# Strassen's seven block products for the first product of the dense experts

## The chip, the cores and the metric

The kernel runs on one core of a Trainium2 chip, with 1 launch. The metric is device time in microseconds (us); lower is better. TensorE (PE in the rows) multiplies, VectorE (DVE), ScalarE (ACT) and GpSimd (POOL) work beside it, and DMA queues move data between HBM and the on-chip memories SBUF and PSUM. PSUM has eight banks of 512 fp32 values per partition; a matrix product accumulates in one bank.

## What is computed

An attention over 2 x 576 tokens feeds two mixtures of experts. The first one sends each token to two of eight experts. The second one, which is changed here, is dense: each of its four experts works on all 1152 tokens.

```python
def _moe2_ref(x, domain_probs, w1, w2):          # x (1152, 512), w1 (4, 512, 1024), w2 (4, 1024, 512)
    p = domain_probs / (domain_probs.sum(-1, keepdims=True) + 1e-09)
    out = np.zeros((N, D), dtype=np.float32)
    for e in range(E):
        h = np.maximum(x @ w1[e], 0.0)
        out += p[:, e:e + 1] * (h @ w2[e])
    return out
```

## The kernel before

Every fp32 operand of a product is held as two parts of type fp32r, a high part (the rounded value) and a low part (the rest). A product is the sum of three: high by high, low by high and high by low. The second mixture keeps its tokens transposed, `xh2` and `xl2`, 128 partitions by 4 pieces of the inner size by 1152 tokens. The arrangement of tokens in nine groups of 128 is called c, and the eight pieces of 128 of the hidden size f.

For each dense expert e there are two stages. The first product (lines 907 to 924) takes 24 steps, 8 pieces f by 3 stretches t of 384 tokens. A step is 12 matmuls of 384 columns into one PSUM bank (L922: 4 inner pieces by 3 products of parts), then ScalarE writes the high part of the ReLU (L923, `h2h`) and VectorE the low part (L924, `h2l`), both reading PSUM. The pool `psg` gives three banks to these steps. The second product (lines 927 to 952) takes nine steps, one for each c: 24 matmuls of 512 columns (8 f by 3, L937), in one of the two banks of `psy`, and one VectorE instruction that adds the result, times the token's weight, to `acc` (L940 for the first expert, L942 for the others). For the last expert GpSimd then sends the rows to the output with an indirect DMA (L946); the last group is cut in two halves of 256 columns.

Weights arrive by `wchunk` (L94): a load of 256 KB into one of five buffers `raw` on SyncE's queue, a cast to the high part on ScalarE (L99), and a subtraction for the low part on GpSimd or VectorE (L102). `w1chunk` has eight buffers (`w1c`), `w2chunk` has eight (`w2c`). The chunks of `w1` for expert e+1 are asked for in the second product of expert e.

The dense expert 0 is special. Its tokens are not all there when it starts: for groups 3 to 8 `fetch` (L713) gathers the two rows that the first mixture left in HBM, into buffers `raw`, with indirect DMAs of GpSimd; `combine` (L726) adds them on VectorE to `x2`; `turn_x2` (L733) transposes a group on TensorE and splits it into `xh2` and `xl2`. These twelve pieces of work stand one by one in front of the first twelve steps of expert 0 (lines 908 to 914), and that expert goes through t in its outer loop, so that tokens 0 to 383 come first.

Each engine works through its own queue in order and waits at the head for what an instruction needs. The order in a queue is set when the program is built, by a planner that takes an instruction early where it holds it ready; it is not always the order of the code.

Of the kernel before, what the change touches and what calls it, by code (L numbers as in the profile page):

```python
# [27 lines left out]
def tile_attention_moe_moe(  # L28
# [65 lines left out]
    def wchunk(src, pool, tag, hi, lo):  # L94
        raw = rawp.tile([P, 512], F32, tag="raw", name="raw")
        nc.sync.dma_start(raw if len(src.shape) == 2 else raw.rearrange("p (k f) -> p k f", k=KC), src)
        t = pool.tile([P, 2, 512], F32R, tag=tag, name=tag)
# [6 lines left out]

    def w1chunk(src, f, hi, lo):
        return wchunk(src[:, f * P:(f + 1) * P].rearrange("(k p) f -> p k f", p=P), w1p, "w1c", hi, lo)
# [400 lines left out]
    psg = ctx.enter_context(tc.tile_pool(name="psg", bufs=3, space=PSUM))  # L507
    psy = ctx.enter_context(tc.tile_pool(name="psy", bufs=2, space=PSUM))
    pstr = ctx.enter_context(tc.tile_pool(name="pstr", bufs=2, space=PSUM))
# [203 lines left out]
    def fetch(c):  # L713
        for k2 in range(2):
            i = 2 * c + k2
            if c > 2:
                ygs[i] = rawp.tile([P, DM], F32, tag="raw", name="yg")
# [71 lines left out]
    for e in range(E1):  # L789
# [69 lines left out]
        for d in range(KC):  # L859
            for f in (2 * d, 2 * d + 1):  # L860
# [30 lines left out]
    uc1 = {0: wc1}  # L891
# [3 lines left out]
    hh = x2p.tile([P, FC, NT * P], F32R, name="h2h")  # L895
    hl = x2p.tile([P, FC, NT * P], F32R, name="h2l")
    acc = x2
    puts = []
    for e in range(E2):
        wc1 = uc1.pop(e)  # L900

        if e == 0:
            order = [(f, t, 3) for t in (0, 3, 6) for f in range(FC)]
        else:
            order = [(f, t, 3) for f in range(FC) for t in (0, 3, 6)]
        wc2 = []
        for i, (f, t, m) in enumerate(order):
            if e == 0 and i < 12:
                if i % 2 == 0:
                    with tc.issue_after(y_adds[0].ins):  # L910
                        fetch(i // 2 + 3)
                        combine(i // 2 + 3)
                else:
                    turn_x2(i // 2 + 3)
            if i % (len(order) // FC) == 0:
                wc2.append(w2chunk(u2[e], len(wc2), nc.scalar, nc.gpsimd))
            o = slice(t * P, (t + m) * P)
            ps = psg.tile([P, 512], F32, tag="g1", name="ps_h2")[:, 0:m * P]
            w = wc1[f].rearrange("p s (k f) -> p s k f", k=KC)
# [90 lines left out]
```

## Time and profile before

| | us |
|---|---|
| median of 3 runs (lowest, highest) | 897.89 (897.16, 898.18) |
| the profiled execution, its own time | 893.92 |
| its span in the trace | 892.1 |
| TensorE busy | 837.3 (94%) |
| VectorE, ScalarE, GpSimd busy | 409.1, 345.0, 343.9 |

The profile is of one execution. A matmul's row in it is longer than the time to the start of the next one, since matmuls overlap; a pace is therefore read from start to start. TensorE's busy time says that it has work, not that it works at its best.

### The profile page before, as it was taken

Reading aid. Unit: us, or ns where it says so; the run is one execution under the profiler, and the core shown is the slowest. Engines: PE = TensorE matmul, PEld = TensorE weight load, DVE = VectorE, ACT = ScalarE, POOL = GpSimd, SP = SyncE. Lnnn points to the kernel's source line nnn. Section 1 sums busy time; section 2 is a strip of 40 time slices with the busy share of each in tenths; the row PEclk is TensorE's granted clock in tenths of the full one; section 3 lists DMA queues with packets and bytes.
Section 4 is the critical chain, followed back from the end, with each engine's and each line's share of the span. In section 5 each row is a group of like instructions: output and inputs, shape, how many; then the busy total and the mean of one; then the engine's idle time right before and its main releaser. Section 6 shows DMA issues by size and latency. Waiting matters only on the chain. (4 is left out here: it accounts for less than half of the span.)

```text
span 892.1 us, 13550 instructions
## 1 busy us (share of the span) xinstructions
PE 837.3 (94%) x5148; PEld 780.3 (87%) x5148; DVE 409.1 (46%) x796; ACT 345.0 (39%) x771; POOL 343.9 (39%) x299
## 2 busy tenths in 40 slices
PE   4899999938979989999999899999999999999996
PEld 3799999938979989999999898899888998899885
DVE  7988888867455435446566521122111221122111
ACT  3778888734325345446432440033103330032100
POOL 6768774647455425334045340052104220040011
PEclk9999999978999989999999999999999999999998
DMA  5423231617446465465373420041103210010011
GB/s 147 112 69 96 70 82 41 181 56 246 144 136 187 141 200 152 141 215 173 116 220 102 136 80 15 0 119 38 34 1 85 58 36 12 1 36 1 12 48 47
DMA packets 94636, 84.42 MB, mean 95 GB/s; under 512 B 14036, under 2 KB 74852, under 8 KB 94564
## 3 DMA queue, kind: packets, MB, share of 16 engines
q1 hardware_dynamic: 89204, 69.34, 26.8%
q0 software_dynamic: 4384, 13.47, 4.7%
q8 instruction: 43, 0.70, 0.3%
q10 hardware_dynamic: 976, 0.66, 0.2%
q14 instruction: 29, 0.24, 0.1%
HBM read 69.66 MB, written 9.66 MB: 89 GB/s over the span
## 5 line engine op out<-in xcount | busy, mean ns | idle before, releaser
L937 PE MATMUL ps_y<-w2c,h2h 128*128 128x512 f32 (+1 forms) x592 | 182.4, 389 | 0.0
L922 PE MATMUL ps_h<-xh,w1c 128*128 128x384 f32 x768 | 149.8, 337 | 3.1 <-DVE h2l L924 3.1
L102 POOL TENSOR_TENSOR w2c<-raw,w2c 128x512 fp32r<-128x512 f32 x60 | 83.0, 1409 | 164.8 <-ACT w2c L99 164.7
L922 PEld LDWEIGHTS ps_h<-xh,w1c 128*128 128x128 f32 x768 | 134.0, 188 | 4.6 <-DVE h2l L924 4.3
L937 PEld LDWEIGHTS ps_y<-w2c,h2h 128*128 128x128 f32 x592 | 110.2, 188 | 25.3
L102 POOL TENSOR_TENSOR w1c<-raw,w1c 128x512 fp32r<-128x512 f32 x60 | 77.3, 1293 | 130.9 <-ACT w1c L99 127.8
L866 PE MATMUL ps_y<-hh,w2c 128*128 128x320 f32 x512 | 124.8, 323 | 2.0 <-PEq L742 2.0
L99 ACT CAST w2c<-raw 128x512 fp32r<-128x512 f32 x96 | 56.4, 619 | 174.3 <-issue 133.6
L937 PE MATMUL ps_y<-w2c,h2l 128*128 128x512 f32 (+1 forms) x296 | 115.2, 389 | 0.0
L924 DVE SCALAR_TENSOR_TENSOR h2l<-ps_h,h2h 128x384 fp32r<-128x384 f32 x96 | 53.3, 557 | 134.5 <-ACT h2h L923 134.5
L923 ACT ACTIVATE h2h<-ps_h 128x384 fp32r<-128x384 f32 x96 | 47.0, 492 | 122.0 <-PE ps_h L922 121.0
L804 PE MATMUL ps_h<-xh,w1c 128*128 128x320 f32 x512 | 89.4, 317 | 3.1 <-DVE hl L806 3.1
L866 PEld LDWEIGHTS ps_y<-hh,w2c 128*128 128x128 f32 x512 | 90.2, 195 | 2.2 <-issue 2.2
L866 PE MATMUL ps_y<-hl,w2c 128*128 128x320 f32 x256 | 82.0, 320 | 3.2 <-DVE x L729 1.7
L804 PEld LDWEIGHTS ps_h<-xh,w1c 128*128 128x128 f32 x512 | 79.4, 193 | 3.9 <-DVE hl L806 3.6
L922 PE MATMUL ps_h<-xl,w1c 128*128 128x384 f32 x384 | 82.4, 336 | 0.0
L942 DVE SCALAR_TENSOR_TENSOR x<-ps_y,tp,x 128x512 f32<-128x512 f32 (+1 forms) x28 | 20.5, 732 | 129.5 <-PE ps_y L937 129.5
L922 PEld LDWEIGHTS ps_h<-xl,w1c 128*128 128x128 f32 x384 | 67.9, 188 | 0.0
L937 PEld LDWEIGHTS ps_y<-w2c,h2l 128*128 128x128 f32 x296 | 55.6, 188 | 12.6
L99 ACT CAST w1c<-raw 128x512 fp32r<-128x512 f32 x88 | 54.2, 616 | 13.6 <-DMA raw<-in_moe_w_dram 13.0
L866 PEld LDWEIGHTS ps_y<-hl,w2c 128*128 128x128 f32 x256 | 50.1, 196 | 4.0 <-DVE x L729 2.0
L293 DVE TENSOR_REDUCE nm<-ps_s 128x1 f32<-128x576 f32 x64 | 48.2, 753 | 10.9 <-PE ps_s L321 10.3
(213 smaller groups left out, 1367.6 us busy)
## 6 DMA issues: line engine op xcount, KB each, us to landing
raw<-in_moe_w_dram SPq DMA_DIRECT2D x192, 256.0 KB
Cs<-C SPq DMA_DIRECT2D x28, 144.0 KB
yd<-yn SPq DMA_DIRECT2D x7, 512.0 KB
xd<-xp SPq DMA_DIRECT2D x4, 576.0 KB
vv<-in_v_dram SPq DMA_DIRECT2D x8, 256.0 KB
qk<-in_q_dram SPq DMA_DIRECT2D x7, 256.0 KB
qk<-in_k_dram SPq DMA_DIRECT2D x7, 256.0 KB
yd<-yn SPq DMA_DIRECT2D x7, 128.0 KB
```

The lines of the kernel that those rows point to most:

```text
L99: hi.copy(t[:, 0, :], raw)
L102: lo.tensor_sub(t[:, 1, :], raw, _f(t[:, 0, :]))
L293: nc.vector.reduce_max(un.nm[:, c:c + 1], ps[:, :, 0:HS], axis=AX.XY, negate=True)
L804: nc.tensor.matmul(ps, w[:, s, kk, :], xx[:, kk, :], start=(n == 0), stop=(n == 3 * KC - 1))
L866: nc.tensor.matmul(ps, wc2[f][:, s, d * P:(d + 1) * P], xx[:, f, :], start=(n == 0), stop=(n == 3 * FC - 1))
L922: nc.tensor.matmul(ps, w[:, s, kk, :], xx[:, kk, o], start=(n == 0), stop=(n == 3 * KC - 1))
L923: nc.scalar.activation(hh[:, f, o], ps, AF.Relu)
L924: vec.scalar_tensor_tensor(hl[:, f, o], ps, 0.0, _f(hh[:, f, o]), op0=ALU.max, op1=ALU.subtract)
L937: nc.tensor.matmul(ps, xx[:, f, c * P:(c + 1) * P], wc2[f][:, s, dd], start=(n == 0), stop=(n == 3 * FC - 1))
L942: vec.scalar_tensor_tensor(acc[:, c, dd], ps, tp[:, c, 8 + e:9 + e], acc[:, c, dd], op0=ALU.mult, op1=ALU.add)
```

## The change

The dense experts 1, 2 and 3 compute their first product by Strassen's scheme in Winograd's form. The matrices are cut in halves: tokens into two halves of 576 (`TH`), the inner size into two of 256, the hidden size into two of 512. Seven products of such blocks and some sums of blocks give the four output blocks. A `unit` takes one piece f and the piece f + 4: 7 products, each of 12 matrix steps (2 inner pieces by 3 products of parts by 2 stretches of 288 tokens), so 84 matmuls of 288 columns. Both stretches go to one PSUM tile of two banks; the pool `psu` has three such tiles, opened when `psg` and `pstr` are closed. The sums of the seven products are made by VectorE in PSUM and in four buffers `tmp`, and one product is copied by ScalarE. There are four units to an expert.

The sums of weights are made by GpSimd in the `raw` buffers (`unit_weights`, four additions of 256 columns) and split as chunks of their own. The sums of tokens are made once, by VectorE, during expert 0 (`token_sums` twice, `token_sum3` twice) and split by ScalarE and VectorE.

The hidden size is now worked off in two sets of two units (`NS` = 2): the first product of a set, then a second product over the set's four pieces, which adds to `acc`. The second product has 12 matmuls to a step, and eighteen steps to an expert. `h2h` and `h2l` have half the size.

Expert 0 keeps its plain first product of 24 steps of 12 matmuls, in the new order of sets: set 0 goes through t in its outer loop with the second product of groups 0 to 2 after the first t. The gathers use the `tmp` buffers and no longer `raw`, the first two before the first step. The low parts of `w2` for expert 0 are made by VectorE and no longer by GpSimd. The last expert of the first mixture asks for the chunks of `w1` in the order 0, 4, 1, 5, 2, 6, 3, 7.

The core of the diff:

```diff
-    for e in range(E2):
-        wc1 = uc1.pop(e)
...
+    def token_sums(q):
+
+        c0, c1 = slice(q * TQ, (q + 1) * TQ), slice(TH + q * TQ, TH + (q + 1) * TQ)
+        b11, b12 = plain(0, c0), plain(0, c1)
+        vec.tensor_tensor(b11, b12, b11, op=ALU.subtract)
+        b22 = plain(2, c1)
+        vec.tensor_tensor(b22, b22, b11, op=ALU.subtract)
+        put_parts(b11, Th[:, 0, :, c0], Tl[:, 0, :, c0])
+        b21 = plain(2, c0)
+        vec.tensor_tensor(b21, b21, b22, op=ALU.subtract)
+        put_parts(b22, Th[:, 1, :, c0], Tl[:, 1, :, c0])
+        put_parts(b21, Th[:, 2, :, c0], Tl[:, 2, :, c0])
...
+    def unit_weights(src, m):
+
+        eng = nc.gpsimd
+        ra, rb = load_raw(w1rows(src, m)), load_raw(w1rows(src, m + FC // 2))
+        lo, hi = slice(0, 256), slice(256, 512)
+        ta, tb = (split_chunk(x, w1p, "w1c", nc.scalar, eng) for x in (ra, rb))
+        eng.tensor_tensor(rb[:, hi], rb[:, lo], rb[:, hi], op=ALU.add)
+        eng.tensor_tensor(rb[:, lo], ra[:, lo], rb[:, lo], op=ALU.subtract)
+        eng.tensor_tensor(ra[:, lo], rb[:, hi], ra[:, lo], op=ALU.subtract)
+        eng.tensor_tensor(ra[:, hi], ra[:, hi], ra[:, lo], op=ALU.subtract)
+        tc_, td_ = (split_chunk(x, w1p, "w1c", nc.scalar, eng) for x in (ra, rb))
...
+        def product(a, b):
+            ps = psu.tile([P, 2, 512], F32, tag="u", name="ps_u")[:, :, 0:TQ]
+            w = blocks[a].rearrange("p s (k f) -> p s k f", k=2)
+            bh, bl = B[b]
+            todo = [(w[:, s, kk], xx[:, kk]) for s, xx in ((0, bh), (1, bh), (0, bl)) for kk in range(2)]
+            for n, (x, y) in enumerate(todo):
+                for j in range(2):
+                    nc.tensor.matmul(
+                        ps[:, j], x, y[:, j * TQ:(j + 1) * TQ], start=(n == 0), stop=(n == len(todo) - 1))
+            return ps
...
+        p1 = temp()
+        nc.scalar.copy(p1, product("11", "11"))
+        both = add(product("S2", "T2"), p1, temp())
+        c11 = add(product("12", "21"), p1)
+        relu_hi(2 * m, h0, c11)
+        v = add(product("S1", "T1"), both, temp())
+        relu_lo(2 * m, h0, c11)
+        p7 = product("S3", "T3")
+        add(p7, both, both)
+        c22 = add(p7, v)
+        relu_hi(2 * m + 1, h1, c22)
+        c12 = add(product("S4", "22"), v)
+        relu_hi(2 * m, h1, c12)
+        relu_lo(2 * m + 1, h1, c22)
+        c21 = add(product("22", "T4"), both)
+        relu_hi(2 * m + 1, h0, c21)
+        relu_lo(2 * m, h1, c12)
+        relu_lo(2 * m + 1, h0, c21)
...
+                if at[0][0] < E2:
+                    prepare = {1: lambda k=at[0]: prepare_unit(k), 4: lambda k=at[1]: prepare_unit(k)}
+            if e > 0:
+                for m in range(MS):
+                    load_w2(2)
+                    unit(m, units.pop((e, s, m)))
+                second(e, s, wc2, range(NT))
+            elif s == 0:
+                for t in (0, 3, 6):
+                    for f in range(2 * MS):
+                        if t == 0:
+                            load_w2(1)
+                        plain_chunk(f, wc1[f], t)
+                        if steps:
+                            steps.pop(0)()
+                    for c in range(3) if t == 0 else ():
+                        second(e, s, wc2, (c,))
+                        steps.pop(0)()
+                    if t == 3:
+                        steps.pop(0)()
+                second(e, s, wc2, range(3, 6))
+                token_sums(0)
+                second(e, s, wc2, range(6, NT))
+            else:
+                for f in range(2 * MS):
+                    load_w2(1)
+                    for t in (0, 3, 6):
+                        plain_chunk(f, wc1[2 * MS + f], t)
+                    if f == 1:
+                        token_sums(1)
+                pctx.close()
+                psu = ctx.enter_context(tc.tile_pool(name="psu", bufs=3, space=PSUM))
+                second(e, s, wc2, range(0, 4))
+                token_sum3(0)
+                second(e, s, wc2, range(4, 7))
+                token_sum3(1)
+                second(e, s, wc2, range(7, NT))
```

In it `TQ` is 288, `NT` is 9, `MS` is 2 and `FC` is 8. `plain` adds a block's high and low parts (one VectorE instruction of 576 columns), `put_parts` splits a sum again (a ScalarE copy and a VectorE subtraction of 576), `add` is a VectorE addition of 576 columns with one operand in PSUM, `relu_hi` and `relu_lo` are the ScalarE and VectorE instructions of L923 and L924 on 576 columns. `prepare` runs after the second product's groups 1 and 4; `second` holds the loop of lines 927 to 952 for one set; `steps` are the `combine` (with the next `fetch`) and `turn_x2` of groups 3 to 8.

## Rows read from the trace of the kernel before

**Rows 1.** Page: the span, busy time by engine, TensorE's granted clock in 40 slices

```profile
span 892.1 us, 13550 instructions
PE 837.3 (94%) x5148; PEld 780.3 (87%) x5148; DVE 409.1 (46%) x796; ACT 345.0 (39%) x771; POOL 343.9 (39%) x299
PEclk9999999978999989999999999999999999999998
```

**Rows 2.** The chain that ended last, in order of time: start, length, what

```profile
583.45 49.92 PE ps_h L922 x288
...
733.68 50.39 PE ps_y L937 x216
```

**Rows 3.** A stretch of expert 1: length, busy time of each engine (instructions), granted clock

```profile
583.90:633.70 49.80, 49.80 (x289) 49.71 (x288) 13.08 (x24) 16.22 (x33) 14.56 (x12) 1.00 0.24 70
```

**Rows 4.** TensorE by time: start, length, what, idle before; two runs of 288 columns

```profile
180.68 0.30 PE L392 MATMUL av<-el,v 128*128 128x288 f32 x1
...
181.60 0.29 PE L394 MATMUL av<-e,v 128*128 128x288 f32 x1
...
182.62 0.29 PE L392 MATMUL av<-el,v 128*128 128x288 f32 x1
...
183.56 0.29 PE L394 MATMUL av<-e,v 128*128 128x288 f32 x1
```

**Rows 5.** VectorE, one line's instructions: ns shortest/median/longest, first and last start

```profile
L924 DVE SCALAR_TENSOR_TENSOR h2l<-ps_h,h2h x96: 542/558/559, 479.2 to 834.6; 128x384 fp32r<-128x384 f32 x96
L729 DVE SCALAR_TENSOR_TENSOR x<-yg,tp,x x18: 732/752/2395, 454.6 to 496.4; 128x512 f32<-128x512 f32 x18
```

**Rows 6.** Groups by line and shape: busy us, mean ns of one, idle before

```profile
L293 DVE TENSOR_REDUCE nm<-ps_s 128x1 f32<-128x576 f32 x64 | 48.2, 753 | 10.9 <-PE ps_s L321 10.3
L294 ACT ACTIVATE eb<-ps_s,nm 128x576 f32<-128x576 f32 x64 | 47.8, 747 | 7.5 <-DVE nm L293 7.4
L222 POOL TENSOR_TENSOR qs<-t,t 128x256 fp32r<-128x256 f32 x1 | 0.7, 726 | 0.7 <-PE ptq L263 0.7
```

**Rows 7.** VectorE by time, in experts 0 and 1

```profile
501.38 1.01 DVE L924 SCALAR_TENSOR_TENSOR h2l<-ps_h,h2h 128x384 fp32r<-128x384 f32 x2
...
587.76 1.02 DVE L924 SCALAR_TENSOR_TENSOR h2l<-ps_h,h2h 128x384 fp32r<-128x384 f32 x2 [3.53 <-ACT h2h L923]
```

**Rows 8.** ScalarE: line L923 in all, then two casts of weights by time

```profile
L923 ACT ACTIVATE h2h<-ps_h x96: 483/492/503, 478.4 to 834.0; 128x384 fp32r<-128x384 f32 x96
491.01 0.62 ACT L99 CAST w2c<-raw 128x512 fp32r<-128x512 f32 x1 [5.03 <-DMA raw<-in_moe_w_dram]
518.92 0.61 ACT L99 CAST w1c<-raw 128x512 fp32r<-128x512 f32 x1
```

**Rows 9.** TensorE by time: expert 0's first product, and where expert 3's ends

```profile
475.38 0.42 PE L922 MATMUL ps_h<-xh,w1c 128*128 128x384 f32 x1
...
479.90 0.60 PE L736 MATMUL pt<-csb,x 128*128 128x128 f32 x4
480.25 0.59 PE L922 MATMUL ps_h<-xl,w1c 128*128 128x384 f32 x2
...
486.17 1.68 PE L922 MATMUL ps_h<-xh,w1c 128*128 128x384 f32 x8 [0.72 <-DVE h2l L924]
...
495.97 1.66 PE L922 MATMUL ps_h<-xh,w1c 128*128 128x384 f32 x8 [1.91 <-DVE h2l L924]
...
532.90 0.39 PE L937 MATMUL ps_y<-w2c,h2h 128*128 128x512 f32 x1
...
833.83 0.39 PE L937 MATMUL ps_y<-w2c,h2h 128*128 128x512 f32 x1
```

**Rows 10.** GpSimd by time: six low parts of weights

```profile
581.84 7.56 POOL L102 TENSOR_TENSOR w2c<-raw,w2c 128x512 fp32r<-128x512 f32 x6
```

**Rows 11.** Stretches in the first mixture, columns as in Rows 3

```profile
326.80:330.40 3.60, 2.13 (x10) 1.75 (x10) 1.19 (x2) 0.94 (x2) 0.00 (x0) 0.65 0.38 142
330.40:334.80 4.40, 4.39 (x17) 4.39 (x18) 0.25 (x1) 0.00 (x0) 0.00 (x0) 0.51 0.21 65
```

More of the change, by code (lines that the diff above doesn't have):

```diff
@@ L716, in fetch @@
             if c > 2:
-                ygs[i] = rawp.tile([P, DM], F32, tag="raw", name="yg")
+                ygs[i] = temp().rearrange("p j t -> p (j t)")[:, 0:DM]
             else:
@@ L890, in tile_attention_moe_moe, with temp @@
     mctx.close()
-    uc1 = {0: wc1}
     x2p = ctx.enter_context(tc.tile_pool(name="x2p", bufs=1))
-    hh = x2p.tile([P, FC, NT * P], F32R, name="h2h")
-    hl = x2p.tile([P, FC, NT * P], F32R, name="h2l")
+    TH = NT * P // 2
+    TQ = TH // 2
+    NS = 2
+    MS = FC // 2 // NS
+    def temp():
+        return x2p.tile([P, 2, TQ], F32, tag="tmp", name="tmp", bufs=4)
     acc = x2
     puts = []
-    for e in range(E2):
-        wc1 = uc1.pop(e)
[L902 to L919, printed above, removed]
-            for n, (s, xx, kk) in enumerate(
-                    [(s, xh2, kk) for kk in range(KC) for s in (0, 1)] + [(0, xl2, kk) for kk in range(KC)]):
-                nc.tensor.matmul(ps, w[:, s, kk, :], xx[:, kk, o], start=(n == 0), stop=(n == 3 * KC - 1))
-            nc.scalar.activation(hh[:, f, o], ps, AF.Relu)
-            vec.scalar_tensor_tensor(hl[:, f, o], ps, 0.0, _f(hh[:, f, o]), op0=ALU.max, op1=ALU.subtract)
-        if e + 1 < E2:
-            uc1[e + 1] = []
-        for c in range(NT):
-            if e + 1 < E2 and c < FC:
-                uc1[e + 1].append(w1chunk(u1[e + 1], c, nc.scalar, nc.gpsimd))
-            cuts = (0, 256, 512) if e == E2 - 1 and c == NT - 1 else (0, 512)
@@ new lines, in relu_hi, with relu_lo, plain_chunk @@
+    def relu_hi(f, o, src):
+        hi = hs[0][:, f, o]
+        nc.scalar.activation(hi if len(src.shape) == 2 else hi.rearrange("p (j t) -> p j t", j=2), src, AF.Relu)
+    def relu_lo(f, o, src):
+        hi, lo = hs[0][:, f, o], hs[1][:, f, o]
+        if len(src.shape) == 3:
+            hi, lo = (x.rearrange("p (j t) -> p j t", j=2) for x in (hi, lo))
+        vec.scalar_tensor_tensor(lo, src, 0.0, _f(hi), op0=ALU.max, op1=ALU.subtract)
+    def plain_chunk(f, w, t):
+        o = slice(t * P, (t + 3) * P)
+        ps = psg.tile([P, 512], F32, tag="g1", name="ps_h2")[:, 0:3 * P]
+        w = w.rearrange("p s (k f) -> p s k f", k=KC)
+        for n, (s, xx, kk) in enumerate(
+                [(s, xh2, kk) for kk in range(KC) for s in (0, 1)] + [(0, xl2, kk) for kk in range(KC)]):
+            nc.tensor.matmul(ps, w[:, s, kk, :], xx[:, kk, o], start=(n == 0), stop=(n == 3 * KC - 1))
+        relu_hi(f, o, ps)
+        relu_lo(f, o, ps)
@@ new lines, in unit, with add @@
+    def unit(m, blocks):
+        def product(a, b):
[8 more added lines that the diff above has]
+            return ps
+        def add(ps, other, dst=None):
+            dst = ps if dst is None else dst
+            vec.tensor_tensor(dst, ps, other, op=ALU.add)
+            return dst
+        p1 = temp()
[16 more added lines that the diff above has]
+        relu_lo(2 * m + 1, h0, c21)
@@ L932, in tile_attention_moe_moe, with second @@
+    def second(e, s, wc2, cs):
+        for c in cs:
+            last = e == E2 - 1 and s == NS - 1
+            cuts = (0, 256, 512) if last and c == NT - 1 else (0, 512)
             for d0, d1 in zip(cuts, cuts[1:]):
```

76 lines of the change are left out of this document (66 added, 10 removed).

## The prediction, made before the changed kernel was run

> **What bounds the kernel now.** I read the page first. TensorE is busy 94% of the span at a granted clock of nine tenths or more nearly everywhere, and no other engine passes 46% [rows 1]. A mean like that hides the stages, so the chain that ended last comes next. In the dense experts it is TensorE and nothing else: the first product of expert 1 is 49.92 us for 288 matmuls, the second one of expert 2 is 50.39 us for 216 [rows 2]. That is 0.173 us for 384 columns and 0.233 us for 512. The stretch of a first product then shows the cover: in 49.80 us VectorE works 13.1 us, ScalarE 16.2 us, GpSimd 14.6 us [rows 3]. So what TensorE saves there is saved in the end, as long as the engines that now get more work keep up.
>
> **Experts 1 to 3, first product.** Removed: 288 matmuls of 384 columns. Added: 4 units of 84 matmuls of 288 columns, 336. The trace has matmuls of 288 columns in runs: seven starts take 0.92 us in one and 0.94 us in another, 0.131 and 0.134 [rows 4]; I take 0.133. 336 x 0.133 = 44.7 us against 49.9: 5.2 us less in each expert, 15.7 us in three. With the two paces as ends the gain is 14.7 to 17.7 us. The second product keeps its matmuls, in 18 groups of 12 (12 x 0.233 = 2.8 us).
>
> **VectorE in the units.** A unit has 11 VectorE instructions of 576 columns, seven additions and four low parts, where 12 of 384 columns (0.558 us [rows 5]) stood for the same two pieces. A reduction of 576 columns out of PSUM took 0.753 us [rows 6], and two L924 in a row take 1.01 us, 0.46 from start to start, 0.1 less than the length of one [rows 7]. So 11 x 0.75 = 8.3 us at most, 7.2 us when packed, beside 84 x 0.133 = 11.2 us of TensorE: it fits in sum, and the question is the order. Four of the 11 write back into PSUM; no row shows that. Nearest is the same read with a result in SBUF, 0.75; below that I see no reason, above it I allow the fixed part once more: from 384 to 576 columns the length grows by 0.195 us, 1.02 ns a column, which leaves 0.558 - 0.39 = 0.17 us for the rest.
>
> With three tiles in `psu`, product n + 3 waits until product n's tile is read out. A product is 12 x 0.133 = 1.6 us, so there are 3.2 us from a product's end to the start of the one that needs its tile. ScalarE starts about 0.2 us after the following matmul's start [rows 8, 9], VectorE 0.1 us after ScalarE's end [rows 5, 8]. Tile 3 is freed by a low part that stands behind the addition on product 4: 1.6 + 0.2 + 0.66 + 0.75 + 0.1 = 3.3 us, 0.1 too late for product 6. The tile of product 5 ends the same way behind the addition on product 6, and delays the next unit's first product by 0.1. At the end of a set, `c21` needs 0.2 + 0.75 + 0.1 + 0.65 (ScalarE's 0.492 for 384, 0.747 for an exponential of 576 [rows 6, 8]) + 0.1 + 0.75 = 2.55 us until its low part is there; the second product wants that after ten matmuls, 2.33 us. So 0.3 + 0.2 = up to 0.5 us for a set of two units. I take 0.4, six sets, 2.4 us. With the dearer PSUM write it is 0.3 more per set (4.2 us in all); if the planner finds something else for TensorE there, nothing.
>
> **ScalarE and GpSimd.** Weights now cost GpSimd 4 subtractions of 512 (7.56/6 = 1.26 us [rows 10]) and 4 additions of 256 (0.73 us [rows 6]) for a unit, 8.0 us, and two low parts of `w2`, 2.5 us: 21 us for a set, which lasts 22.3 + 25.2 = 47.5 us. ScalarE has about 3.3 us of PSUM reads and 6 casts of 0.62, 7 us for a unit. Both are covered. GpSimd's six subtractions ran from 581.84 to 589.40 and VectorE's L924 beside them kept its 1.02 us for two [rows 7, 10]: instructions with one operand in PSUM, as all 11 are, are not held up. Loads are as many as before (8 chunks of `w1`, 8 of `w2` to an expert). Nine more additions to `acc` in each expert, 0.75 us each in groups of 2.8 us, hide in the same way.
>
> **Expert 0.** Its first product runs from 475.38 to 532.90, 57.5 us [rows 9], for 49.9 us of matmuls and 27 transposes at 0.35 us for four [rows 9], 2.4 us. 5.2 us are lost to waits on gathers, loads and VectorE, 0.72 and 1.91 us of them in the two rows shown [rows 9], while ScalarE stood 5.03 us at a cast whose buffer `raw` was late [rows 8]. The change gives the gathers other buffers, issues two before the first step, and puts three groups of the second product (8.4 us) ahead of where tokens 384 and on are wanted. I expect those waits gone. Against that VectorE gets the token sums, 28 instructions of 576 columns, about 0.75 us each, 21 us in all, beside the low parts of `w2`. Ten of them in one go (7.5 us) behind an addition to `acc` would cost what exceeds two groups less an addition, 7.5 - (5.6 - 0.75) = 2.7 us, and ten amid first-product steps 2 us or so (three free banks, 3 x 2.1 us). But the trace shows the planner moving work ahead: a cast of the next expert's `w1` runs at 518.92, inside the first product [rows 8], though the code asks for it in the second. Spread like that the sums cost little. These instructions read SBUF twice; such a one (L729) took up to 2.4 us, against 0.75 as a rule, while GpSimd worked too [rows 5]. So expert 0 lies between 5.2 us gained and 5 us lost; I take 2 us of new waits, 3.2 us gained.
>
> **The end** is unchanged: two halves, an addition and an output DMA each. The DMAs now come every 2.8 us, GpSimd needs about 1 us for one.
>
> **Rivals.** (A) The part work blocks ScalarE. Casts of the weight sums wait for GpSimd's chain (2 subtractions, 4 additions: 2.5 + 2.9 = 5.4 us) at the head of ScalarE's queue, and behind them stand the copy of product 1 and the ReLUs. TensorE has 3.2 us of tiles; beyond that a cast costs up to 2.2 us and more if the cast's load is late too. For it: ScalarE did stand 5.03 us so in expert 0, and TensorE with it [rows 8, 9]. Against it: the work is asked for in the second product, where ScalarE has nothing urgent. At 12 units x 2.2 us = 26 us the kernel would be 10 us slower, 908; it is slower as soon as a unit loses more than (15.7 + 3.2 - 2.4)/12 = 1.4 us. (B) VectorE becomes the bound of the units, if its instructions on PSUM in place take much more than a row shows. At 1 us each for 11 a unit is 11 us and just hides; what it loses in order then is about 0.7 us a unit, 8 us, and the kernel is at 889. At 1.14 us nothing would be left. (C) Weight loads set TensorE's pace. A load lasts longer than a 288-column matmul and TensorE's loads are busy 49.71 of 49.80 us at 384 columns [rows 3]; if a matmul could not start faster than 0.17 us, 336 of them are 57 us, 21 us more in all, 916. The runs at 0.133 had one load for each matmul as well, so I give it little. (D) The clock. In a stretch where TensorE was busy only 2.13 of 3.60 us the granted clock was 0.65, and in the 4.4 us behind it 0.51, the lower level of 1.2 GHz [rows 11]; at the wait of 1.91 us in expert 0 the matmuls behind kept their pace [rows 9]. Waits of 0.1 us are far from that; but units at half the clock would take 11 us more each. The Trainium skill speaks against this change here: "TensorE: Matmul & The Clock Gate", section "A second HAM failure mode: psum-queue depth-cycling", reports a kernel that cycled through PSUM banks, idled briefly between groups and saw its clock fall and rise again and again. By that rule the units could lose up to 12 x 11 us and the kernel would be near 1000; the rows of this case, with three banks cycled in every first product at a clock of 1.00 [rows 3], do not bear it out.
>
> **How the numbers follow.** The sum is -15.7 + 2.4 - 3.2 = -16.5 us. The profiled execution took 893.92 us, with a span of 892.1, and would take 877.4; the median of the runs shown stands 3.97 us above it, and the same difference from 897.89 gives 881.4. Without new waits and with all of expert 0's old ones gone it is -17.7 - 5.2 = -22.9, 875. With the dear writes, the slow pace and 5 us lost in expert 0 it is -14.7 + 4.2 + 5 = -5.5, 892.4. Chances: the forecast (875 to 892.4, in which B's mild form lies) 0.76, A 0.12, of which a quarter ends between 892 and 896, C 0.03, D 0.02, B in the hard form 0.04, faster than 875 0.03. The range 875 to 894 holds about 8 in 10. About 0.2% (1.8 us) is what a measurement of this kernel can tell from no change: faster 0.81, within it 0.03, slower 0.16.
>
> **What would show it.** Right: the distance from the start of a unit's first matmul to the next unit's is near 11.2 us and its matmuls follow each other every 0.13 us; waits of TensorE on VectorE are under 0.3 us; the first to last matmul of an expert takes near 96 us instead of 100.3; expert 0 takes some 105 us instead of 107.9. Wrong: in A the rows of ScalarE's casts have GpSimd as releaser with microseconds behind them; in B VectorE is busy nine tenths or more in the units; in C the matmuls' starts are 0.17 us apart with no wait; in D the granted clock in the units is below 1; and if the token sums run in blocks, expert 0's second product has waits of several us on `acc`.

## The result, and the profile after

The changed kernel takes 908.4 us (median of 4 runs, 907.12 to 910.01), the kernel before on the same chip 897.52 (4 runs, 892.24 to 898.18): 1.0135 times as long, with an interval of 1.0093 to 1.0177. It is slower, by 1.35%. The forecast was 881.4 with a range of 875 to 894; the time is the one that rival A gave, 908.

The page of the changed kernel (span, busy time by engine):

```profile
span 906.1 us, 14046 instructions
...
PE 831.0 (92%) x5280; PEld 767.2 (85%) x5280; DVE 513.3 (57%) x928; ACT 366.5 (40%) x791; POOL 402.8 (44%) x363
```

TensorE does have less to do, 831.0 us for 837.3 [rows 1], and the span is 14.0 us longer: TensorE stands and waits, 8% of the span for 6%. The averages of the other engines are far from full, as before. So the time went into order, not into volume. Split by stage, from the start of one first product to the start of the next (the last stage ends with the span):

| us | before | after |
|---|---|---|
| start of expert 0 | 475.38 | 471.97 |
| expert 0 | 107.9 | 113.1 |
| experts 1 to 3 | 308.8 | 321.0 |
| of it: five sets that prepare another one | | 53.80, 53.54, 52.11, 53.73, 52.39 |
| of it: the last set, with the output | | 55.5 |

What TensorE waited for in experts 1 to 3 (line waited for: us in total, times, longest), then its weight loads, and then ScalarE, of the changed kernel:

```profile
PE ps_y L1039 <- ACT h2h L971: 12.7, 5, 2.6
PE ps_u L1000 <- DVE h2l L977: 5.0, 5, 1.2
PE ps_u L1000 <- ACT tmp L1010: 1.0, 5, 0.3
...
PEld ps_y L1039 <- ACT h2h L971: 15.1, 6, 3.0
...
ACT w1c L105 <- POOL raw L964: 19.4, 10, 3.2
ACT w2c L105 <- DMA raw<-in_moe_w_dram: 15.3, 15, 2.0
```

In the kernel before, this view lists no wait of TensorE there. Now it waits five times for the ReLU (L971) of the last piece, once in each set but the last, five times about 1 us for low parts, and five times some 0.2 us for the copy of product 1 (L1010). ScalarE itself waits ten times for GpSimd's last addition of weights (L964), once for each unit that these experts prepare, and fifteen times for a load of `w2`.

The chain that ended last, in order of time (start, length, what), shows how the one leads to the other at the end of expert 1's first set:

```profile
606.57 0.63 ACT w1c L105
...
607.27 1.30 POOL w1c L108
...
611.10 0.74 POOL raw L964
...
611.86 0.62 ACT w1c L105
612.48 0.55 ACT h2h L971
...
613.53 0.56 ACT h2h L971
...
614.14 22.82 PE ps_y L1039 x90
```

It is to be read as a relay for the next unit's weights: a cast, a subtraction, four additions (three are left out), the next cast. Only then come the two ReLUs that TensorE needs now, with one more cast between them (left out). Before the change the chain was a row of TensorE pieces here [rows 2]. ScalarE's queue a little earlier and at the same place (start, length, what, idle before and its cause):

```profile
597.33 0.62 ACT L105 CAST w2c<-raw 128x512 fp32r<-128x512 f32 x1 [1.94 <-DMA raw<-in_moe_w_dram]
597.85 0.65 ACT L971 ACTIVATE h2h<-ps_u 128x576 fp32r<-128x576 f32 x1
...
606.57 0.62 ACT L105 CAST w1c<-raw 128x512 fp32r<-128x512 f32 x1 [1.79 <-PE ps_u L1000]
...
611.86 0.62 ACT L105 CAST w1c<-raw 128x512 fp32r<-128x512 f32 x1 [3.22 <-POOL raw L964]
612.38 0.64 ACT L971 ACTIVATE h2h<-ps_u 128x576 fp32r<-128x576 f32 x1
```

The cast of 611.86 stands at the head for 3.22 us; the ReLU behind it starts with no wait of its own, so its operand had been there. The relay's first cast, at 606.57, had itself waited 1.79 us for TensorE: the eight buffers `w1c` hold just the two units of the running set (four chunks to a unit), and one came free only then. The cast of 597.33, of `w2`, stood 1.94 us for its load with a ReLU behind it; the low part of that ReLU comes at 598.53 and TensorE, which wants its PSUM tile, has a wait of 1.16 us until 599.43. So there are two casts that block, one behind GpSimd (the 12.7 us on L971), one behind a load (the 5.0 us on L977). TensorE, by time, at the end of the set:

```profile
609.53 0.40 PE L1039 MATMUL ps_y<-w2c,h2l 128*128 128x512 f32 x1
...
611.15 0.40 PE L1039 MATMUL ps_y<-w2c,h2h 128*128 128x512 f32 x1
614.14 0.88 PE L1039 MATMUL ps_y<-w2c,h2h 128*128 128x512 f32 x2 [2.59 <-ACT h2h L971]
...
618.12 0.40 PE L1039 MATMUL ps_y<-w2c,h2l 128*128 128x512 f32 x1
```

Eight matmuls of the second product run, then TensorE waits 2.59 us, and then the next ten take 3.98 us (614.14 to 618.12) where ten at 0.233 take 2.33. The granted clock says why (length, busy time of PE, PEld, DVE, ACT, POOL with instructions, clock, DMA share, GB/s; the second and third line are the 4 us behind the same wait in the next two sets, the last line is the two units of the last set, which prepares nothing):

```profile
614.00:618.00 4.00, 3.86 (x10) 2.99 (x11) 1.51 (x2) 0.09 (x1) 1.06 (x1) 0.57 0.50 131
...
667.59:671.59 4.00, 4.00 (x12) 3.08 (x13) 1.49 (x2) 0.00 (x0) 0.93 (x1) 0.70 0.47 131
721.24:725.24 4.00, 4.00 (x17) 3.11 (x18) 1.60 (x3) 0.00 (x0) 0.93 (x1) 1.00 0.44 131
...
850.81:873.30 22.49, 22.49 (x171) 22.41 (x170) 14.52 (x20) 5.69 (x9) 0.00 (x0) 1.00 0.01 1
```

After this wait TensorE works near its lower level of 1.2 GHz for about four microseconds. Not each such wait brings that: the five waits on the ReLU last 2.54 to 2.59 us, and over the 4 us behind them the clock is 0.57, 0.70, 1.00, 0.69 and 1.00. The two sets in which it stays at 1.00 are the two short ones, 52.11 and 52.39 us. Why an equal wait brings it in one set and not in another, no run here shows. The loss of the first set adds up: its second unit takes 13.03 us (596.50 to 609.53) instead of 11.2, 1.83 (of which the wait behind the late load of `w2` is 1.16, and 0.16 is a wait on the copy of product 1, which stood behind casts of weight sums); from 611.38, when another matmul could have started, to the next one it is 2.76 (614.14); the slow pace costs 3.98 - 2.33 = 1.65. That is 6.2 us; against two units of 11.2 and 108 matmuls of 0.233, 47.6 us, the set of 53.80 us lost 6.2. In the last set, where GpSimd has nothing to do, two such units take 22.5 us with no wait:

```profile
850.65 1.23 PE L1000 MATMUL ps_u<-xh,w1c 128*128 128x288 f32 x8
...
862.08 1.11 PE L1000 MATMUL ps_u<-xh,w1c 128*128 128x288 f32 x7
```

11.43 us from unit to unit with one 512-column matmul of the second product (0.23) among them: 11.2, as forecast. The durations are as assumed as well: a low part of 576 columns takes 0.755 us and a ReLU 0.650, where the prediction had 0.75 and 0.65. The write back into PSUM in place costs 10 ns more than a result in SBUF (by line: busy us, mean ns, idle before):

```profile
L1006 DVE TENSOR_TENSOR ps_u<-ps_u,tmp 128x576 f32<-128x576 f32 x48 | 36.6, 763 | 14.4 <-PE ps_u L1000 14.4
...
L1006 DVE TENSOR_TENSOR tmp<-ps_u,tmp 128x576 f32<-128x576 f32 x36 | 27.1, 753 | 19.0 <-PE ps_u L1000 19.0
```

In expert 0 of the changed kernel, TensorE and ScalarE by time and GpSimd's first gather of group 3:

```profile
482.09 1.11 PE L746 MATMUL pt<-csb,x 128*128 128x128 f32 x4 [3.25 <-DVE x L739]
521.59 0.50 PE L1039 MATMUL ps_y<-w2c,h2h 128*128 128x512 f32 x1 [2.13 <-DVE x L1043]
...
518.04 0.62 ACT L105 CAST w1c<-raw 128x512 fp32r<-128x512 f32 x1 [3.18 <-POOL raw L964]
...
519.14 0.48 ACT L971 ACTIVATE h2h<-ps_h 128x384 fp32r<-128x384 f32 x1
...
473.75 2.54 POOL L732 DMA_INDIRECT tmp<-yd,ti  x1 [17.16 <-ACT w2c L105]
```

The granted clock from each of the two waits on (columns as above):

```profile
481.00:486.50 5.50, 4.41 (x20) 4.38 (x21) 4.23 (x8) 1.09 (x3) 4.53 (x4) 0.69 0.70 206
521.60:526.00 4.40, 4.40 (x12) 3.47 (x13) 4.40 (x7) 0.00 (x0) 0.41 (x1) 0.61 0.32 101
```

There are two waits, and the clock fell behind both (0.69 and 0.61). The first one is a transpose that waits for gathered rows; the gathers start at 473.75, behind the start of the expert, where the kernel before had those of groups 3 and 4 out from 458.29 to 464.69. The second one is again a cast for expert 1's weights (3.18 us at the head of ScalarE's queue), with a cast of token sums and a ReLU of expert 0 behind it. TensorE waits there for an addition to `acc` on VectorE (L1043), in whose queue the low part of that ReLU and the token sums stand ahead of it. By the two lines on the clock some 1.7 us were lost behind each wait (5.50 x 0.31 and 4.40 x 0.39); before the change the clock was 1.00 over all of expert 0.

### The profile page after: what moved, and what is told of

Read it like the earlier page. It is cut to its first block, busy times and chain, and to the rows that moved or that the text cites. A ratio compares the mean times of both kernels' runs of the same rounds, so it can differ in the third digit from the quotient of the medians.

```text
span 906.1 us, 14046 instructions
## 1 busy us (share of the span) xinstructions
PE 831.0 (92%) x5280; PEld 767.2 (85%) x5280; DVE 513.3 (57%) x928; ACT 366.5 (40%) x791; POOL 402.8 (44%) x363
## 4 chain that ended last, share of the span: by engine, by line
PE 42%; POOL 9%; DMA 5%; issue 3%; ACT 3%; DVE 1%; POOLq 0%; ACTq 0%; DVEq 0%
PE ps_y L1039 18%; PE ps_y L876 7%; PE ps_u L1000 5%; PE ps_h L814 5%; PE ps_h L986 5%; DMA raw<-in_moe_w_dram 4%; POOL w2c L108 2%; POOL w1c L108 2%; ACT w1c L105 1%; ACT h2h L971 1%; POOL raw L962 1%; POOL raw L961 1%; POOL raw L963 1%; POOL raw L964 1%; POOL out_dram L1049 1%
## 5 line engine op out<-in xcount | busy, mean ns | idle before, releaser
L1039 PE MATMUL ps_y<-w2c,h2h 128*128 128x512 f32 (+1 forms) x584 | 188.1, 402 | 14.9 <-ACT h2h L971 12.7
L108 POOL TENSOR_TENSOR w1c<-raw,w1c 128x512 fp32r<-128x512 f32 x84 | 109.4, 1310 | 92.0 <-ACT w1c L105 91.8
L1039 PEld LDWEIGHTS ps_y<-w2c,h2h 128*128 128x128 f32 x584 | 111.6, 193 | 43.0 <-ACT h2h L971 15.1
L1045 DVE SCALAR_TENSOR_TENSOR x<-ps_y,tp,x 128x512 f32<-128x512 f32 (+1 forms) x64 | 47.5, 742 | 121.6 <-PE ps_y L1039 121.6
L105 ACT CAST w1c<-raw 128x512 fp32r<-128x512 f32 x112 | 68.6, 617 | 65.1 <-PE ps_u L1000 27.3
L814 PEld LDWEIGHTS ps_h<-xh,w1c 128*128 128x128 f32 x512 | 79.3, 193 | 3.4 <-DVE hl L816 3.1
L1000 PE MATMUL ps_u<-xh,w1c 128*128 128x288 f32 x384 | 59.6, 298 | 1.0 <-ACT tmp L1010 1.0
L977 DVE SCALAR_TENSOR_TENSOR h2l<-ps_u,h2h 128x576 fp32r<-128x576 f32 x48 | 36.2, 755 | 38.5 <-ACT h2h L971 38.3
L1000 PEld LDWEIGHTS ps_u<-xh,w1c 128*128 128x128 f32 x384 | 53.9, 188 | 3.2 <-ACT tmp L1010 2.2
L108 DVE TENSOR_TENSOR w2c<-raw,w2c 128x512 fp32r<-128x512 f32 x44 | 44.3, 1036 | 20.4 <-ACT w2c L105 20.4
L303 ACT ACTIVATE eb<-ps_s,nm 128x576 f32<-128x576 f32 x64 | 47.8, 748 | 7.7 <-DVE nm L302 7.6
L1000 PE MATMUL ps_u<-Th,w1c 128*128 128x288 f32 x288 | 44.6, 298 | 5.0 <-DVE h2l L977 5.0
```

Source lines behind the costliest of these rows:

```text
L105: hi.copy(t[:, 0, :], raw)
L108: lo.tensor_sub(t[:, 1, :], raw, _f(t[:, 0, :]))
L303: nc.scalar.activation(e.rearrange("p (a s) -> p a s", a=2), ps[:, :, 0:HS], AF.Exp, bias=un.nm[:, c:c + 1], accum_out=un.rs[:, c:c + 1],)
L814: nc.tensor.matmul(ps, w[:, s, kk, :], xx[:, kk, :], start=(n == 0), stop=(n == 3 * KC - 1))
L977: vec.scalar_tensor_tensor(lo, src, 0.0, _f(hi), op0=ALU.max, op1=ALU.subtract)
L1000: nc.tensor.matmul(ps[:, j], x, y[:, j * TQ:(j + 1) * TQ], start=(n == 0), stop=(n == len(todo) - 1))
```

## The experiments

The runs were made on three more chips, each beside the kernel before, whose median was 888.91, 890.11 and 893.22 us there. So a time is compared with the kernel before on its own chip, and across chips the lengths of the stages are compared. In the table "sets" is the sum of the five sets that prepare another one, 5 x 47.64 = 238.2 us where TensorE never waits; the last set takes 55.5 us in all of them.

| us | median | before beside it | ratio | expert 0 | sets | experts 1 to 3 |
|---|---|---|---|---|---|---|
| before | | | | 107.9 | | 308.8 |
| changed | 908.4 | 897.52 | 1.0135 | 113.1 | 265.6 | 321.0 |
| e1_gate | 884.0 | 888.91 | 0.9941 (0.9918 to 0.9963) | 110.4 | 248.6 | 304.0 |
| e2_pool | 884.57 (one run) | 888.91 | | 112.4 | 244.1 | 299.6 |
| e3_raw | 908.36 (one run) | 888.91 | | 112.3 | 265.1 | 320.7 |
| e4_nosums | 901.6 (one run) | 888.91 | | 108.7 | 264.0 | 319.6 |
| after_again | 904.35 | 890.11 | 1.0165 (1.011 to 1.022) | 113.5 | 265.4 | 320.9 |
| e5_w2 | 874.87 | 890.11 | 0.9842 (0.9799 to 0.9885) | 108.7 | 238.2 | 293.7 |
| e6_turns | 875.89 | 890.11 | 0.985 (0.9817 to 0.9883) | 110.6 | 238.2 | 293.6 |
| e7_raw | 883.05 | 893.22 | 0.9883 (0.9818 to 0.9947) | 108.7 | 238.2 | 293.7 |
| e8_nosums | 881.08 (one run) | 893.22 | | 106.6 | 238.2 | 293.7 |

**e1_gate: the casts may not stand ahead of the ReLUs.** The casts for the next set take their place in ScalarE's queue behind the last ReLU of the running set. Nothing else is changed.

```diff
-        nc.scalar.activation(hi if len(src.shape) == 2 else hi.rearrange("p (j t) -> p j t", j=2), src, AF.Relu)
+        hold["hi"] = nc.scalar.activation(
+            hi if len(src.shape) == 2 else hi.rearrange("p (j t) -> p j t", j=2), src, AF.Relu)
...
-                    units[key] = unit_weights(u1[key[0]], key[1] * MS + key[2])
+                    with tc.issue_after(hold["hi"].ins):
+                        units[key] = unit_weights(u1[key[0]], key[1] * MS + key[2])
```

> The changed kernel, with one edge more: the casts of the next set's weights on ScalarE are queued behind the last ReLU of the running set. Nothing else moves. If ScalarE's queue is the cause (casts of weight sums that wait for GpSimd, with ReLUs behind them), each of the five sets that prepare a next one falls from 53.1 us to 47.5 to 48.5 us, the wait of 2.1 us in expert 0 goes as well, and the time falls by 25 to 30 us, to 878 to 884. If the units are slow by the order of VectorE's instructions or by the three PSUM tiles, nothing of that is touched and the time stays within 3 us of 907. If the next set's weights now come too late, the first unit of a set starts with a wait of several us.

Measured: 884.0 us, 0.9941 times the kernel before. The sets fall from 265.6 to 248.6 us, so 17 of the 27.4 us that were lost there come back through the order of one queue, with the same instructions. That is less than was expected: the sets take 48.7 to 51.9 us and not 47.5 to 48.5. The wait of 2.1 us in expert 0 is gone, as expected. What is left of TensorE's waits in experts 1 to 3:

```profile
PE ps_u L1003 <- DVE h2l L980: 7.8, 5, 2.6
```

TensorE and ScalarE by time in the second set:

```profile
641.77 1.29 PE L1003 MATMUL ps_u<-Th,w1c 128*128 128x288 f32 x8 [2.56 <-DVE h2l L980]
...
643.69 2.12 PE L1003 MATMUL ps_u<-xh,w1c 128*128 128x288 f32 x8
...
639.67 0.62 ACT L105 CAST w2c<-raw 128x512 fp32r<-128x512 f32 x1 [3.27 <-DMA raw<-in_moe_w_dram]
640.20 1.18 ACT L973 ACTIVATE h2h<-ps_u 128x576 fp32r<-128x576 f32 x2
```

The wait on the ReLU behind GpSimd is gone, the other one is left and longer: a cast of `w2` waits 3.27 us for its load, two ReLUs stand behind it, TensorE waits 2.56 us and then takes 2.12 us for eight matmuls that otherwise take 1.23. The loads of `w2` for the running set come one at a time here. Four of the five `raw` buffers hold the next set's weights, which now wait longer for their casts; that this is why the loads follow each other so slowly is read from the order of the buffers, and e5_w2 tests what follows from it.

**e2_pool: ScalarE is spared instead.** The high parts of the two sums of weights are made by GpSimd, which makes the sums; ScalarE has no cast that waits for GpSimd's additions.

```diff
-        tc_, td_ = (split_chunk(x, w1p, "w1c", nc.scalar, eng) for x in (ra, rb))
+        tc_, td_ = (split_chunk(x, w1p, "w1c", eng, eng) for x in (ra, rb))
```

> The changed kernel, with the high parts of the weight sums cast by GpSimd and no longer by ScalarE, so that no ScalarE instruction waits for GpSimd's additions; GpSimd has 1.25 us more per unit. If the waiting ScalarE instruction is the cause, the ReLUs come in time, a set falls to about 48 us, and the time to 880 to 886. If GpSimd's own load is the cause (its chain is too long), the time stays or rises by up to 12 us, to 907 to 920.

Measured: 884.57 us in one run; the sets take 244.1 us, 21.5 less. TensorE's waits, first in experts 1 to 3, then in expert 0:

```profile
PE ps_u L1000 <- DVE h2l L977: 4.0, 4, 1.2
...
PE ps_y L1039 <- DVE x L1043: 2.8, 2, 1.6
```

The waits of 2.6 us on the ReLU are gone, though GpSimd has more to do than before. Two kernels that have in common only that no cast on ScalarE waits for the additions ahead of a ReLU gain 17 and 21.5 us in the same place: that wait is the cause of most of the loss in the sets. The rival that VectorE is the bound of the units can't give this, since neither kernel touches VectorE's work. Expert 0 is another matter: it stays at 112.4 us here, and TensorE still waits 2.8 us for additions to `acc` (L1043), though no cast on ScalarE waits for GpSimd's additions. So the waiting cast isn't the only cause of the wait on L1043 in the changed kernel. In e2 token sums stand ahead of these additions in VectorE's queue, slow beside GpSimd's work (see the last section); the gate, which takes that work out of their way, and e4, which has no sums, are both free of the wait.

**e3_raw: the first gathers go into the buffers that they had before.** A test of the first wait in expert 0.

```diff
-                ygs[i] = temp().rearrange("p j t -> p (j t)")[:, 0:DM]
+                ygs[i] = (rawp.tile([P, DM], F32, tag="raw", name="yg") if c < 5 else
+                          temp().rearrange("p j t -> p (j t)")[:, 0:DM])
```

> The changed kernel, with the first two gathers (groups 3 and 4) in the raw buffers again, as before, so that they need not wait for the memory of the first mixture. If that memory is what made the first gather start at 473.8 us instead of 463.4, TensorE's wait of 3.3 us before the transposes of group 3 and the slow clock behind it go: expert 0 falls by 4 to 6 us, the time to 901 to 904. If the loads of w2 now wait for raw buffers instead, or if the token sums are what costs, expert 0 stays at 113 us and the time at 907.

Measured: 908.36 us in one run, expert 0 112.3 us; the gain that was expected of expert 0 isn't there. The wait on L739 went, and others took its place: one of 2.4 us at a transpose ahead of expert 0, and two on low parts of 2.3 us together. The gathers of the later groups still start only at 475.40.

**e4_nosums: what the sums of tokens cost.**

```diff
-                    "T1": (Th[:, 0], Tl[:, 0]), "T2": (Th[:, 1], Tl[:, 1]), "T4": (Th[:, 2], Tl[:, 2]),
+                    "T1": (xh2[:, 0:2, h0], xl2[:, 0:2, h0]), "T2": (xh2[:, 2:4, h0], xl2[:, 2:4, h0]),
+                    "T4": (xh2[:, 2:4, h1], xl2[:, 2:4, h1]),
...
-                token_sums(0)
...
-                    if f == 1:
-                        token_sums(1)
...
-                token_sum3(0)
...
-                token_sum3(1)
```

> The changed kernel without the token sums: the blocks T1, T2, T3, T4 are replaced by blocks of the tokens themselves, so the 28 VectorE and 8 ScalarE instructions are left out and the result is another one. The matmuls are the same in number and size. If the sums hold up TensorE in expert 0, that expert loses the wait of 2.1 us and some of its 113 us, and the time is 903 to 905; if they are hidden, the time stays within 1 us of 907. The sets of experts 1 to 3 should stay at 53 us under either.

Measured: 901.6 us in one run. Expert 0 takes 108.7 us, 4.4 less than in the changed kernel; the sets keep their loss (264.0). So the sums are worth at most some 4 us in expert 0 and nothing behind it. Of the 4.4 us, 2.13 are the wait on L1043, which is gone, and some 1.7 the lower clock behind it.

**after_again: the changed kernel once more, on the second chip.**

> The changed kernel again, on the chip of the two runs beside it, since the kernel before took 897.5 us on one chip and 888.9 us on another. If the loss belongs to the change and not to the chip, it stays 1 to 2% slower than the kernel before on the same chip; its five sets with a preparation last about 53 us each, and expert 0 113 us.

Measured: 904.35 us, 1.0165 times the kernel before, with the same stages within 0.5 us (2 runs). The result doesn't hang on the chip.

**e5_w2: the gate, and `w2` asked for one set earlier.** In the running set's second product, behind the same gate, so that no load of `w2` is left to the units.

```diff
+                def prepare_w2(key):
+                    w2next[key] = []
+                    with tc.issue_after(hold["hi"].ins):
+                        load_w2(4, e=key[0], s=key[1], wc2=w2next[key])
...
-                    prepare = {1: lambda k=at[0]: prepare_unit(k), 4: lambda k=at[1]: prepare_unit(k)}
+                    prepare = {1: lambda k=at[0]: prepare_unit(k), 4: lambda k=at[1]: prepare_unit(k),
+                               5: lambda k=at[0][:2]: prepare_w2(k)}
...
-                    load_w2(2)
```

> The gated kernel, with the chunks of w2 for the next set asked for in the running set's second product too, behind the weights of w1 and behind the same gate; so ScalarE has nothing but the copy of product 1 and the ReLUs to do while units run. In the gated kernel five sets still took 48.7 to 51.9 us, with casts of w2 waiting for loads (up to 3.3 us) ahead of ReLUs. If that wait is what is left of the loss, the sets fall to 47.6 us with nothing but some 0.3 us of waits, 6 to 9 us in all, and the time to 875 to 878 where the gated kernel has 884. If the three PSUM tiles and VectorE's order are what is left, the sets stay at 49 us. If GpSimd (21 us per set) does not get done within the second product (25 us), the first unit waits, and nothing or less than nothing is gained.

Measured: 874.87 us, 0.9842 times the kernel before; this version beats both kernels. All five sets take 47.64 us. The first of them (columns as above):

```profile
579.37:627.01 47.64, 47.64 (x277) 42.60 (x276) 22.73 (x31) 12.94 (x22) 20.96 (x20) 1.00 0.13 38
```

All waits of TensorE's weight loads in experts 1 to 3 (its matmuls have none), and ScalarE's on GpSimd:

```profile
PEld ps_y L1042 <- ACT h2h L973: 1.2, 6, 0.2
...
ACT w1c L105 <- POOL raw L964: 55.0, 10, 6.0
```

The last line is the one to learn from. ScalarE waits for GpSimd ten times as before, and far longer, 55.0 us for 19.4, and it costs nothing, since no ReLU stands behind these casts. VectorE works 22.73 us of a set, ScalarE 12.94, GpSimd 20.96: that the extra work fits beside TensorE was right.

**e6_turns: expert 0's transposes of groups 3 to 5 later.** As e5, and the gathered rows get more time before TensorE wants them.

```diff
-    steps = [g for c in range(3, NT) for g in (lambda c=c: join(c), lambda c=c: turn_x2(c))]
+    order = [(join, 3), (join, 4), (join, 5), (join, 6), (turn_x2, 3), (turn_x2, 4), (turn_x2, 5),
+             (turn_x2, 6), (join, 7), (turn_x2, 7), (join, 8), (turn_x2, 8)]
+    steps = [lambda g=g, c=c: g(c) for g, c in order]
```

> As the run above, and in expert 0 the transposes of groups 3 to 5 stand behind the first steps of the second product, no longer in the first product's steps, so that TensorE does not stand at the transposes of group 3 until its gather lands. If that wait (3.2 us) and the slow clock behind it are lost time, expert 0 falls from 110 us by 3 to 5 us and the time to 870 to 875. If TensorE then waits as long for the same gathers a little later, expert 0 stays at 110 us.

Measured: 875.89 us, no different from e5, and expert 0 is 1.9 us longer. The wait on L739 is gone; three on VectorE's low parts take its place, 3.4 us in all:

```profile
PE ps_y L1042 <- DVE h2l L980: 3.4, 3, 2.5
```

**e7_raw: e5 with the edit of e3.**

> The kernel with both weights behind the gate, and the first two gathers in the raw buffers. Its expert 0 took 108.7 us, with a wait of 2.6 us for group 3's gather and a slower clock behind it, about 2 us more. If these are lost only because the gather buffers lie in the first mixture's memory, expert 0 falls to 104 to 106 us and the time from 875 to 871 to 873. If the later groups, whose gathers still wait for that memory, come late as well, it stays at 108 us or above and the time at 875.

Measured: 883.05 us, 0.9883 times the kernel before on its chip, so not better than e5. The gathers of groups 3 and 4 now go out early, from 458.36 to 464.25, and the planner then takes the additions that combine their rows (L740) into the first mixture. There VectorE stands at the head of its queue until the rows land, and behind it wait the additions (L852) that TensorE's transposes of the first tokens need. VectorE, then TensorE:

```profile
466.88 0.75 DVE L740 SCALAR_TENSOR_TENSOR x<-yg,tp,x 128x512 f32<-128x512 f32 x1 [1.67 <-DMA yg<-yd,ti]
...
468.97 0.85 DVE L852 SCALAR_TENSOR_TENSOR x<-pt_y,tp,x 128x128 f32<-128x128 f32 x3
...
469.88 0.81 PE L747 MATMUL pt<-csb,x 128*128 128x128 f32 x4 [2.56 <-DVE x L852]
```

The clock was 0.57 over the 4 us behind it. It is the same fault as in the changed kernel, on another engine: early work that waits, ahead of urgent work. Expert 0 is as long as in e5 (108.7): it has the same 24 transposes, and in place of the wait for group 3 there are two on low parts, 2.3 us together. The gathers of the later groups still start only at 481.03, behind the expert's start at 479.25. Three ways of handling these gathers only moved this wait.

**e8_nosums: e5 with the edit of e4.**

> The kernel with both weights behind the gate, without the token sums (blocks of the tokens stand in for T1 to T4, 36 instructions left out, another result). If the planner spreads the sums over VectorE's idle time at no cost to TensorE, expert 0 stays within 1 us of 108.7 us; if they hold TensorE up, it falls by 2 to 5 us. In the changed kernel without the gate, leaving them out took 4.4 us from expert 0; if that came from the wait at ScalarE that they lengthened, nothing of it is left here.

Measured: 881.08 us in one run. Expert 0 takes 106.6 us, 2.1 less than in e5, and the sets are unchanged at 47.64. Most of the 2.1 us isn't the work of the sums. In both kernels TensorE waits for the rows of group 3 (L739), 2.60 us in e5 and 2.53 in e8, before e5 makes a sum; behind that wait the clock fell in e5 and not in e8 (first e5, then e8, columns as above):

```profile
480.00:486.00 6.00, 5.82 (x27) 5.61 (x28) 4.57 (x9) 2.10 (x4) 4.78 (x5) 0.73 0.75 217
...
486.00:492.00 6.00, 4.76 (x30) 4.73 (x31) 5.03 (x9) 1.50 (x3) 4.58 (x5) 1.00 0.63 192
```

By the first line e5 lost 6.00 x (1 - 0.73) = 1.6 us there. From 500 to 520, while the sums are made in e5, TensorE was busy throughout at a clock of 1.00. So with ScalarE's queue in order the sums cost some 0.5 us at most, by one trace of each kernel; in the changed kernel without that order 4.4.

## Why the prediction was wrong

**The step that failed** is "Both are covered", in the paragraph on ScalarE and GpSimd, with the 0.12 that rival A got from it. The sum was right: 7 us of ScalarE in a unit of 11.2 us fit, and e5 shows them fitting. But a sum of busy time says nothing of an engine that works its queue in order and stands at the head of it. Against A the prediction said that "the work is asked for in the second product, where ScalarE has nothing urgent". That is where the code asks for it, not where the planner puts it. The row that says so was among those that were shown: a cast of the next expert's `w1` at 518.92, inside a first product [rows 8]. It was used to argue that the token sums will be spread, and left out where the casts were weighed. There it was harmless, for the row shows no wait; after the change it waits for a chain of 4.6 us on GpSimd (607.27 to 611.86). The rows for A's price were there as well, 5.03 us of ScalarE at a cast in expert 0 with TensorE behind it [rows 8, 9].

**The price of A** was put at 12 units x 2.2 = 26 us, as a wait for PSUM tiles once in each unit. Measured are 27.4 us in five sets of two units, 5.5 for a set, and they are made otherwise. The wait behind GpSimd's chain comes once in a set, not once in a unit, and it stops the second product, which wants the last ReLU, not a tile: 12.7 us. Late loads of `w2` add 5.0, the copy of product 1 adds 1.0, and the lower clock behind three of the five waits some 1.65 each, which wasn't in A's price; some 3.7 us, 0.7 for a set, are in no wait that is listed. That 908 was met so closely is in part luck. A's sum held -3.2 for expert 0, where +5.2 was measured, and +2.4 for PSUM tiles, where nothing was, and expert 0 happened to start 3.4 us earlier than in the profile of before: -3.4 + 5.2 - 15.1 + 27.3 is the 14.0 us of the spans.

**The main term was right.** -15.7 for 336 matmuls of 288 columns: e5 takes 293.7 us for experts 1 to 3 where the kernel before takes 308.8, -15.1, with 11.2 us to a unit. The gain is in the changed kernel too, and 27.4 us are paid on top of it: 321.0 = 293.7 + 27.3.

**The waits on PSUM tiles** (+2.4) were too dear. In e5 TensorE's matmuls don't wait in the units; the planner puts a matmul of the second product between two units and takes the pieces first that are ready, which the prediction had named as the case of nothing. The write into PSUM in place, bounded by 0.75 and 0.92 us, measured 0.763. Rivals B and C fell with it: VectorE was busy 14.52 of 22.49 us in two units, and in e5 the 12 matmuls of a product took 1.60 us.

**Expert 0** was mis-sized: -3.2 forecast, +5.2 measured, 113.1 us for 107.9. Two waits of TensorE, 5.4 us, stand where the kernel before had 3.1, and the clock behind them took some 3.4 where it had taken nothing; a lower clock in expert 0 stood in no term. Mechanism A has a part in it: with the gate alone the expert takes 110.4 us, in e5 108.7. How much of that is the cast that waited and how much GpSimd's additions beside the token sums stays open, since the gate moves both. The sums by themselves cost some 0.5 us at most in e5 (2 was taken). "I expect those waits gone" was wrong: the old ones went, and a wait on gathered rows of 3.25 us came. The gathers' new buffers were to free them from the loads; instead the first gather went out 15 us later than before, at 473.75 and not at 458.29. That `tmp` lies in memory which the first mixture holds until its end would give this, but it is only argued; e3, e6 and e7 moved the wait without removing it. The reckoning of the old loss has a slip as well: the trace has 24 transposes in this stretch, six groups of four, and not 27, so that 2.1 us go to them and not 2.4, and 5.5 us and not 5.2 were lost. In e8, where the clock is 1.00 throughout, 106.6 us stand against 102.4 of matmuls and transposes; 2.5 of the rest are the wait on the gathered rows, and 1.7 are open.

**Rival D** was in part right, in a form that had no price. It isn't the cycling of PSUM tiles: with three tiles cycled through the units the clock in e5 is 1.00 in whole sets, so the rule of the Trainium skill that was weighed ("TensorE: Matmul & The Clock Gate", section "A second HAM failure mode: psum-queue depth-cycling") found nothing to act on here. But in the changed kernel five of seven waits of 2.13 to 3.25 us were followed by several microseconds near the lower level, so that such a wait cost more than it lasted, 1.65 us more in the set shown. Two of them, of 2.54 us, and the wait of 2.53 us in e8 were not, nor was the one from which the prediction judged, 1.91 us [rows 9]. What decides it stays open.

**The sign** hung on one queue. With the order mended, e5's ratio applied to the 897.52 us of the first chip gives about 883 us, an estimate (0.9842 x 897.52), near the 881.4 of the forecast: the arithmetic was that of the kernel that the change could have been. Two errors cancel there in part: in e5 expert 0 is 0.8 us longer than before the change, not 3.2 shorter, and the 2.4 us for PSUM tiles are not paid.

## What to carry to other kernels

When a change gives an engine work for later stages, don't ask only whether its busy time fits: write down what stands in its queue behind each instruction that waits for another engine, and take the place from where a planner puts such work in the trace, not from the code. The cheap repair is to queue early work behind the last urgent instruction of the stage, along with everything else that waits in that queue, loads included; a long wait there is free once nothing urgent is behind it. And price a wait of TensorE of two or three microseconds with what the clock may take behind it: in some of these runs nothing, in others about as much again.

## What the runs showed of the hardware

VectorE with both operands in SBUF and GpSimd at work in SBUF held each other up. In expert 0 of the changed kernel (VectorE, then GpSimd, by time):

```profile
513.68 1.29 DVE L928 TENSOR_TENSOR tmp<-xh,xl 128x576 f32<-128x576 f32 x1
514.90 1.29 DVE L941 TENSOR_TENSOR tmp<-tmp 128x576 f32<-128x576 f32 x1
...
514.44 1.14 POOL L962 TENSOR_TENSOR raw<-raw 128x256 f32<-128x256 f32 x1
515.65 1.14 POOL L963 TENSOR_TENSOR raw<-raw 128x256 f32<-128x256 f32 x1
```

The starts follow each other every 1.21 to 1.22 us on both engines. In e5, where GpSimd does nothing while the sums are made, the same VectorE instructions take 0.75 us. In the units, where VectorE has one operand in PSUM, 576 columns take it 0.753 to 0.763 us and an addition of GpSimd 0.73 to 0.74. The page "SBUF — State Buffer" of the Trainium skill, section "SBUF: two separate sides", tells of a pair of ports that the two engines lock in turns, for a VectorE instruction with two inputs in SBUF beside one of GpSimd that reads SBUF; the trace agrees in kind (1.21 us from start to start, against 0.67 for VectorE in e5 and 0.81 for GpSimd in the units), and no row shows the lock itself. It lengthens the very chain for which ScalarE waited 3.18 us in expert 0.

The starts of expert 0 lie between 467 and 479 us in kernels that run nearly the same code up to there. That spread, of the chips and of the runs, is larger than what several of the experiments were to show, and only the stage lengths made them readable.
